# Turning keys, queries and tokens by the DMA crossbar instead of TensorE in a chunked-attention and feed-forward kernel

## The chip, the cores and the metric

The kernel runs on one core of a Trainium2 chip. The metric is the time of one execution on the device in microseconds (us); lower is better. A profile of one execution belongs to each kernel: it shows when each engine worked on which instruction and what it waited for. The engines are TensorE (PE, with its weight loads as PEld), VectorE (DVE), ScalarE (ACT), GpSimd (POOL) and SyncE (SP), which here only issues DMA transfers. DMA transfers are issued by SyncE (queue SPq) and by GpSimd (POOLq).

## The reference

Two stages. The first is attention over chunks of 32 queries: each chunk sees 8 memory keys, 16 keys to its left, its own 32 and 8 to its right. There are 4 batches, 8 heads, 768 positions and a head size of 64. The second is a layer norm and a two-layer feed-forward (512 to 2048 to 512) with a residual.

```python
for c in range(nc):                              # 24 chunks of 32
    l_start = max(0, c_start - 16); r_end = min(S, c_end + 8)
    k_full = np.concatenate([mem_k, k[:, :, l_start:r_end]], axis=2)
    v_full = np.concatenate([mem_v, v[:, :, l_start:r_end]], axis=2)
    scores = scale * np.matmul(q_c, k_full.transpose(0, 1, 3, 2))
    scores = scores - np.max(scores, axis=-1, keepdims=True)
    a = np.exp(scores); a = a / (np.sum(a, axis=-1, keepdims=True) + 1e-09)
    out[:, :, c_start:c_end] = np.matmul(a, v_full)
# x = attention's output, (4, 768, 512)
xn = (x - mu) / np.sqrt(var + 1e-06) * g_ln
out = x + np.maximum(xn @ w_ch1, 0.0) @ w_ch2
```

All inputs and outputs are fp32; the kernel casts to fp16 while it loads.

## The kernel before

Two chunks make a group of 64 queries; there are 12 groups in a batch. A group's scores come from 96 key columns: 8 of memory and 88 around the 64 queries. The keys stand turned (head size on partitions) in `KT`, with two heads on the 128 partitions, four pairs `j`. The queries stand turned in `QZ`, each head in its own half of the partitions and zeros in the other half, so that one matmul gives both heads of a pair. Two groups make a tile of 128 tokens, three tiles a unit of 384 tokens; there are 8 units, two for each batch. While unit `u` goes through the feed-forward, the three tiles of unit `u + 1` go through attention, at steps that a plan lays down. A unit has 28 steps: 16 `up` steps (four matmuls each, then a ReLU, by VectorE at even steps and ScalarE at odd ones), then 12 `down` steps (four matmuls each).

Turning is TensorE's, with an identity, into PSUM; a copy then takes it to SBUF:

```python
def turn_kq(pv, src, j, n):
    for r in range(8):
        for par in range(2):
            nc.tensor.matmul(
                out=pv[64 * par : 64 * par + 64, n * r : n * r + n],
                lhsT=src[0:n, 2 * j + par, r, :], rhs=identity[0:n, 0:n],
                is_transpose=True, start=True, stop=True, tile_position=(0, 64 * par))

def kq_block(b, j, g0, g1, kind):        # keys and queries of two head pairs, j and j + 1
    ...
    for i in range(2):
        turn_kq(as16(pk[:, i, :]), k16[b % 2], j + i, 96)
    for i in range(2):
        turn_kq(as16(pq[i]), q16[b % 2], j + i, 96)
    def keep(i):
        keep_k(...)                      # VectorE: PSUM to KT
        for par in range(2):
            keep_q(nc.scalar.copy, ...)  # ScalarE: PSUM to QZ
    ...

def turn_x(u, i, t, kind="att"):         # a tile's tokens, 128 x 512
    pv = as16(slot("att")[:, 0, :]) if kind == "att" else as16(slot("mm")[:, :])
    for dt in range(4):
        nc.tensor.matmul(
            out=pv[:, 128 * dt : 128 * dt + 128],
            lhsT=xn[t % 3][:, 128 * dt : 128 * dt + 128], rhs=identity,
            is_transpose=True, start=True, stop=True)
    nc.scalar.copy(out=xT[u % 2][:, :, 128 * i : 128 * i + 128], in_=free(pv, 0, [[128, 4], [1, 128]]))
```

Attention of a tile is `scores` (8 matmuls, then two exponentials by ScalarE), `values` (16 matmuls), `norm` (VectorE: reciprocal, scaling with the row sum, mean, and `xn`, the centred row times the gain `g_row`), `turn_x`, and `root` (ScalarE squares, GpSimd makes `rstd`). The feed-forward and the end of a tile:

```python
def up(u, n, hc):
    p = slot("mm")[:, 0 : 128 * n]
    for dt in range(4):
        nc.tensor.matmul(out=p, lhsT=free(w, i, [[4, 128]]), rhs=xT[u % 2][:, dt, 0 : 128 * n], ...)
    if hc % 2: nc.scalar.activation(out=rT[hc][...], in_=p, func=ACTF.Relu)
    else:      nc.vector.tensor_scalar(out=rT[hc][...], in0=p, scalar1=0.0, op0=ALU.max, ...)

def down(t, i, part):
    for hc in range(4 * part, 4 * part + 4):
        nc.tensor.matmul(out=p, lhsT=rT[hc][:, 128 * i : 128 * i + 128], rhs=w2c[hc // 4][:, hc % 4, :], ...)
    if part == 3:
        nc.vector.scalar_tensor_tensor(out=osb[t % 3], in0=p, scalar=rstd[t % 9], in1=xs[t % 9], ...)
        nc.sync.dma_start(out=out[...], in_=osb[t % 3])
```

PSUM has two buffers `att` of two banks each and four `mm` of one. `stay_busy(n)` puts `n` filler matmuls of 512 columns on TensorE. The part of the plan that the change touches:

```python
late = ((16, 19, 19, 22), (17, 21, 21, 24), (19, 23, 23, 26))   # scores, values, norm, turn_x
if u == 0:
    at(1, clear_q, 1, 0); at(5, clear_q, 1, 1); at(8, clear_v, 1); at(11, clear_k, 1)
    for j in (0, 2):
        at(10 + j, kq_block, 0, j, 6, NG, "att"); at(11 + j, keep_rest)
    ...
    attend(late)
elif u == 1:
    for j in (0, 2):
        at(5 + 3 * j, kq_block, 1, j, 0, NG, "att"); at(7 + 3 * j, keep_rest)
    ...
    attend(late)
elif u in (2, 4):
    attend(((1, 8, 8, 12), (4, 8, 10, 14), (11, 17, 17, 21)))
    b = u // 2 + 1
    for j, step in ((0, 17), (2, 23)):
        at(step, kq_block, b, j, 0, NG, "mm"); at(step, keep_rest)
    for h in range(H):
        at(2 + 2 * h, load_v_head, b, h)
    at(21, mem_cols, b); at(21, v_mem, b); at(22, v_around, b)
elif following:                                                   # units 3, 5, 6
    attend(((12, 17, 17, 21), (14, 17, 17, 22), (18, 23, 23, 26)))
```

Of the kernel before, what the change touches and what calls it, by code (L numbers as in the profile page):

```python
# [15 lines left out]
def kernel(  # L16
# [12 lines left out]
    nc = tc.nc  # L29
# [4 lines left out]
    KR = 96  # L34
    KC = NG * KR + 32
    HD = 80
# [21 lines left out]
    w2c = [sb.tile([128, 4, 512], FP16, name=f"w2c{i}") for i in range(4)]  # L58
    k16 = [sb.tile([96, H, 8, 64], FP16, name=f"k16_{i}") for i in range(2)]
    q16 = [sb.tile([96, H, 8, 64], FP16, name=f"q16_{i}") for i in range(2)]  # L60
    V = [sb.tile([128, NG, H, HD], FP16, name=f"V{i}") for i in range(2)]
    KT = [sb.tile([128, 4, KC], FP16, name=f"KT{i}") for i in range(2)]
    QZ = [sb.tile([128, 4, NG, 2, 64], FP16, name=f"QZ{i}") for i in range(2)]
    AT = [sb.tile([128, 2, H, 64], FP16, name=f"AT{i}") for i in range(3)]
# [30 lines left out]
    def as16(t):  # L95
        return t.bitcast(FP16)
# [13 lines left out]
    def load_v_group(b, g):  # L110

        lo, hi = max(64 * g - 16, 0), min(64 * g + 72, S)
        r = 24 + lo - 64 * g
        nc.gpsimd.dma_start(  # L114
            out=V[b % 2][r : r + hi - lo, g, :, 0:64],
            in_=dram(v, b * H * HS + lo * D, [[64, hi - lo], [HS, H], [1, 64]]),
        )

    def load_v_head(b, h):
        nc.gpsimd.dma_start(  # L120
            out=V[b % 2][24:88, :, h, 0:64],
            in_=dram(v, (b * H + h) * HS, [[64, 64], [64 * 64, NG], [1, 64]]),
        )

    def v_around(b):

        vt = V[b % 2]
        nc.sync.dma_start(out=vt[8:24, 1:NG, :, :], in_=vt[72:88, 0 : NG - 1, :, :])
        nc.sync.dma_start(out=vt[88:96, 0 : NG - 1, :, :], in_=vt[24:32, 1:NG, :, :])

    def v_mem(b):
        src = memv16[:, b, :, :]
        nc.sync.dma_start(
            out=V[b % 2][0:8, :, :, :],
            in_=bass.AP(tensor=src.tensor, offset=src.offset,
                        ap=[list(src.ap[0]), [0, NG], [1, H * HD]]),
        )
# [26 lines left out]
    def mem_cols(b):  # L164
        src = memKT[:, 4 * b : 4 * b + 4, :]
        nc.vector.tensor_copy(
            out=free(KT[b % 2], 0, [[KC, 4], [KR, NG], [1, 8]]),
            in_=bass.AP(tensor=src.tensor, offset=src.offset,
                        ap=[list(src.ap[0]), [8, 4], [0, NG], [1, 8]]),
        )  # L170
# [13 lines left out]
    def keep_k(pv, b, j, n, g0, g1, copy=nc.vector.tensor_copy):  # L184

        for ga, gb in ((0, 1), (1, NG - 1), (NG - 1, NG)):
            ga, gb = max(ga, g0), min(gb, g1)
            if ga < gb:
                lo = 0 if ga == 0 else 8 * ga - 2
                m = 10 if gb == NG else 8 * ga + 9 - lo  # L190
                copy(  # L191
                    out=free(KT[b % 2], j * KC + 24 + 32 * ga + 8 * lo,
                             [[KR, gb - ga], [8, m], [1, 8]]),
                    in_=free(pv, lo, [[8, gb - ga], [1, m], [n, 8]]),
                )

    def keep_q(copy, pv, b, j, par, n, g0, g1):


        rows = slice(64 * par, 64 * par + 64)  # L200
        copy(  # L201
            out=free(QZ[b % 2][rows, j, g0, par, :], 0, [[128, g1 - g0], [8, 8], [1, 8]]),
            in_=free(pv[rows, :], 8 * g0, [[8, g1 - g0], [1, 8], [n, 8]]),
        )
# [24 lines left out]
    def keep_rest():  # L229
        kept_later.pop(0)()  # L230

    def scores(b, t):
        p = slot("att")
        a = AT[t % 3]
        for gg in range(2):
            g = 2 * t + gg
            for j in range(4):
                nc.tensor.matmul(  # L238
                    out=p[:, gg, 128 * j : 128 * j + 128],
                    lhsT=KT[b % 2][:, j, KR * g : KR * g + 128],  # L240
                    rhs=QZ[b % 2][:, j, g, :, :],
                    start=True, stop=True,
                )
# [48 lines left out]

    def turn_x(u, i, t, kind="att"):
        pv = as16(slot("att")[:, 0, :]) if kind == "att" else as16(slot("mm")[:, :])
        for dt in range(4):
# [72 lines left out]
    def clear_k(i):  # L368
        nc.vector.memset(KT[i][:, :, 8:24], 0.0)
        nc.vector.memset(KT[i][:, :, NG * KR - 8 : KC], 0.0)  # L370

# [32 lines left out]
    for h in (0, 4):  # L404
        for which in range(2):
            load_kq(0, which, 0, CUT, h, h + 4)
    keep(counts[:, 0:1], counts[:, 0:1], 24, 0.0)
    keep(counts[:, 1:2], counts[:, 1:2], -88, 0.0)
    make_identity(nc, identity)
# [7 lines left out]
    mem_cols(0)  # L417
    pg = slot("mm")[:, :]
    nc.tensor.matmul(out=pg, lhsT=ones32, rhs=g_one, start=True, stop=True)
    nc.scalar.copy(out=g_row, in_=pg)  # L420
    v_mem(0)
# [5 lines left out]
    nc.gpsimd.memset(zero2[:, 1:2], -NEG)  # L427
    keep(band[:, 0:1], zero2[:, 0:1], -64, NEG)
    keep(band[:, 1:2], zero2[:, 0:1], 40, NEG)
    keep(zero2[:, 1:2], zero2[:, 1:2], -8, 0.0)  # L430
    nc.gpsimd.tensor_tensor(out=band[:, 1:2], in0=band[:, 1:2], in1=zero2[:, 1:2], op=ALU.add)
    for g in range(4, 6):
# [47 lines left out]
    scores(0, 1)  # L480
    stay_busy(5)
    values(0, 0)
# [20 lines left out]
    for u, tiles in enumerate(units):  # L503
# [6 lines left out]

        def attend(steps):

            for i, (s0, s1, s2, s3) in enumerate(steps):
# [3 lines left out]
                at(s2, norm, t % 6, t % 9)  # L517
                at(s3, turn_x, u + 1, i, t % 6)
                at(min(s3 + 1, 27), root, t % 6, t % 9)

        late = ((16, 19, 19, 22), (17, 21, 21, 24), (19, 23, 23, 26))
        if u == 0:
            at(1, clear_q, 1, 0)
            at(5, clear_q, 1, 1)
            at(8, clear_v, 1)
            at(11, clear_k, 1)
            for j in (0, 2):
# [5 lines left out]
            for g in range(6):  # L533
                at(15, load_v_group, 1, g)
            attend(late)
            at(26, mem_cols, 1)
            at(26, v_mem, 1)
        elif u == 1:
# [3 lines left out]
            for g in range(6, NG):  # L542
                at(0, load_v_group, 1, g)
            for which in range(2):
                at(1, load_kq, 2, which)
            attend(late)
        elif u in (2, 4):
            attend(((1, 8, 8, 12), (4, 8, 10, 14), (11, 17, 17, 21)))
            b = u // 2 + 1
            for j, step in ((0, 17), (2, 23)):  # L550
                at(step, kq_block, b, j, 0, NG, "mm")
                at(step, keep_rest)
            for h in range(H):
                at(2 + 2 * h, load_v_head, b, h)
            at(21, mem_cols, b)
            at(21, v_mem, b)
            at(22, v_around, b)
        elif following:
            attend(((12, 17, 17, 21), (14, 17, 17, 22), (18, 23, 23, 26)))
            if u == 3:  # L560
                for which in range(2):
                    at(2 + which, load_kq, 3, which)
        for step in range(16 + 4 * n):
# [43 lines left out]
```

## Time and profile before

| | |
|---|---|
| time, median of 3 runs | 233.54 us (230.09 to 233.69) |
| time of the profiled execution, its span | 230.39 us, 228.7 us |
| TensorE clock granted | 1.00 |
| DMA queue of GpSimd (`q0`) | 45680 packets, 14.23 MB |
| DMA queue of SyncE (`q1`) | 4602 packets, 7.54 MB |
| output writes of 256 KB, issue to landing | 4.0 us, median |

A profile is read from the whole to the part. The span runs from the first instruction to the last. Busy time of an engine is the time in which it had an instruction; of TensorE it says little about speed, because matmuls are pipelined, and two that follow each other overlap in the records: the mean duration of a matmul is longer than the step to the next. The chain of waits is followed back from the last instruction, at each step to what released it; its rows are the time that sets the end. Lines are named by their number in the kernel: L176 is a transpose in `turn_kq`, L296 one in `turn_x`, L319 a matmul of `up`, L336 one of `down`, L238 of `scores`, L258 of `values`, L310 a filler.

### The profile page before, as it was taken

How to read it: one execution, taken by the hardware profiler on the slowest of the kernel's cores; microseconds unless marked ns; L12 is line 12 of the kernel's file. 1: busy time of each engine (PE TensorE's matmuls, PEld its weight loads, DVE VectorE, ACT ScalarE, POOL GpSimd, SP SyncE). 2: the span in 40 equal slices, each digit the busy share in tenths (PEclk: the TensorE clock that was granted, in tenths of full speed). 3: DMA queues.
4: the chain of work that ended last, by engine and by line, in shares of the span. 5: the costliest groups of instructions: out<-in, count | busy, mean ns of one | idle time of the engine just before them, and what ended most of it. 6: DMA issues, size and time to landing. Idle time of an engine off the chain costs nothing.

```text
span 228.7 us, 5500 instructions
## 1 busy us (share of the span) xinstructions
PE 221.6 (97%) x2289; PEld 137.2 (60%) x2289; DVE 127.2 (56%) x290; ACT 119.0 (52%) x228; POOL 68.5 (30%) x125
## 2 busy tenths in 40 slices
PE   7989989999999999999999999999999999999993
PEld 2555666557755676556765676556764566556553
DVE  6856882585728548674436557774336532663222
ACT  3565548364884567654356458653446345533200
POOL 7982426968300460440001461310001100030000
PEclk9999999999999999999999999999999999999999
DMA  4999999999995190559911290553001200111012
GB/s 78 181 144 206 211 193 177 178 185 210 122 201 119 67 128 3 37 99 132 241 25 49 90 108 1 37 109 112 0 3 46 92 3 0 47 49 46 0 46 96
DMA packets 50307, 22.13 MB, mean 97 GB/s; under 512 B 37817, under 2 KB 46777, under 8 KB 50234
## 3 DMA queue, kind: packets, MB, share of 16 engines
q0 software_dynamic: 45680, 14.23, 58.4%
q1 hardware_dynamic: 4602, 7.54, 11.0%
q8 instruction: 18, 0.29, 0.6%
q14 instruction: 7, 0.06, 0.1%
HBM read 28.48 MB, written 6.29 MB: 152 GB/s over the span
## 4 chain that ended last, share of the span: by engine, by line
PE 87%; DVE 6%; DMA 3%; issue 2%; POOL 1%; DVEq 0%; POOLq 0%
PE mm L336 35%; PE mm L319 33%; PE att L238 5%; PE att L258 3%; PE att L176 3%; DMA k<-in_k_dram 3%; PE att L296 2%; PE mm L176 2%; PE mm L354 2%; DVE rT L327 1%; DVE xs L269 1%; PE mm L310 1%; DVE xn L278 1%; DVE QZ L374 1%; DVE V L380 1%
## 5 line engine op out<-in xcount | busy, mean ns | idle before, releaser
L319 PE MATMUL mm<-xT,w1c 128*128 128x384 f16 x512 | 88.3, 326 | 0.0
L336 PE MATMUL mm<-w2c,rT 128*128 128x512 f16 x368 | 87.4, 379 | 0.0
L319 PEld LDWEIGHTS <-w1c 128*128 128x128 f16 x512 | 56.6, 113 | 24.5 <-issue 0.3
L327 DVE TENSOR_SCALAR rT<-mm 128x384 f16<-128x384 f32 x64 | 35.3, 554 | 34.7 <-PE mm L319 34.5
L336 PEld LDWEIGHTS <-rT 128*128 128x128 f16 x368 | 33.7, 98 | 33.7
L325 ACT ACTIVATE rT<-mm 128x384 f16<-128x384 f32 x64 | 31.2, 489 | 35.8 <-PE mm L319 33.9
L287 POOL TENSOR_SCALAR veps<-squares 128x1 f32<-128x1 f32 x24 | 4.5, 188 | 115.9 <-ACT junk L284 101.2
L245 ACT ACTIVATE AT<-att,band 96x512 f16<-96x512 f32 x48 | 30.1, 677 | 17.0 <-PE att L238 16.6
L343 DVE SCALAR_TENSOR_TENSOR osb<-mm,rstd,xs 128x512 f32<-128x512 f32 x23 | 17.2, 749 | 30.7 <-PE mm L336 20.1
L114 POOL DMA_DIRECT2D V<-in_v_dram x24 | 21.4, 898 | 10.4 <-DMA w1c<-in_moe_w_ch_dram 5.7
L301 ACT COPY xT<-att 128x512 f16<-128x512 f16 x21 | 12.2, 581 | 22.4 <-PE att L296 22.4
L191 DVE COPY KT<-att 128x80 f16<-128x80 f16 (+3 forms) x44 | 18.4, 480 | 2.4 <-PE att L176 2.4
L278 DVE SCALAR_TENSOR_TENSOR xn<-xs,nmean,g_row 128x512 f16<-128x512 f32 x24 | 18.0, 752 | 0.9
L201 ACT COPY QZ<-mm 64x768 f16<-64x768 f16 (+1 forms) x18 | 13.6, 757 | 7.9 <-PE mm L176 7.7
L284 ACT ACTIVATE junk<-xs,nmean 128x512 f16<-128x512 f32 x24 | 17.4, 724 | 0.1
L268 DVE RECIPROCAL rec<-att 128x8 f32<-128x8 f32 x24 | 4.8, 202 | 22.2 <-PE att L258 22.2
L269 DVE SCALAR_TENSOR_TENSOR xs<-att,rec 128x512 f32<-128x512 f32 x24 | 16.6, 691 | 0.8
L238 PE MATMUL att<-QZ,KT 128*128 128x128 f16 x192 | 14.8, 219 | 0.9 <-ACT AT L245 0.7
L238 PEld LDWEIGHTS <-KT 128*128 128x128 f16 x192 | 12.6, 98 | 4.6 <-issue 1.5
L201 ACT COPY QZ<-att 64x384 f16<-64x384 f16 (+1 forms) x20 | 12.0, 598 | 5.9 <-PE att L176 5.7
L291 POOL TENSOR_TENSOR rstd<-veps,mhalf 128x1 f32<-128x1 f32 x24 | 13.3, 553 | 2.0
L120 POOL DMA_DIRECT2D V<-in_v_dram x16 | 12.1, 763 | 0.3 <-issue 0.3
(63 smaller groups left out, 141.6 us busy)
## 6 DMA issues: line engine op xcount, KB each, us to landing
out_dram<-osb SPq DMA_DIRECT2D x23, 256.0 KB, 4.0
w1c<-in_moe_w_ch_dram POOLq DMA_DIRECT2D x4, 512.0 KB, 10.9
w2c<-in_moe_w_ch_dram POOLq DMA_DIRECT2D x4, 512.0 KB, 14.4
V<-in_v_dram POOLq DMA_DIRECT2D x20, 88.0 KB, 9.8
k<-in_k_dram POOLq DMA_DIRECT2D x2, 768.0 KB, 10.0
q<-in_q_dram POOLq DMA_DIRECT2D x2, 768.0 KB, 13.1
V<-in_v_dram POOLq DMA_DIRECT2D x16, 96.0 KB, 3.2
k<-in_k_dram POOLq DMA_DIRECT2D x3, 256.0 KB, 6.3
```

The source lines that it names most:

```text
L114: nc.gpsimd.dma_start(out=V[b % 2][r : r + hi - lo, g, :, 0:64], in_=dram(v, b * H * HS + lo * D, [[64, hi - lo], [HS, H], [1, 64]]),)
L191: copy(out=free(KT[b % 2], j * KC + 24 + 32 * ga + 8 * lo, [[KR, gb - ga], [8, m], [1, 8]]), in_=free(pv, lo, [[8, gb - ga], [1, m], [n, 8]]),
L201: copy(out=free(QZ[b % 2][rows, j, g0, par, :], 0, [[128, g1 - g0], [8, 8], [1, 8]]), in_=free(pv[rows, :], 8 * g0, [[8, g1 - g0], [1, 8], ...
L238: nc.tensor.matmul(out=p[:, gg, 128 * j : 128 * j + 128], lhsT=KT[b % 2][:, j, KR * g : KR * g + 128], rhs=QZ[b % 2][:, j, g, :, :], start ...
L245: nc.scalar.activation(out=free(a, 32 * c, [[512, 2], [64, 8], [1, 32]], KR), in_=free(p, 32 * c, [[512, 2], [64, 8], [1, 32]], KR), func= ...
L269: nc.vector.scalar_tensor_tensor(out=x.rearrange("p (h d) -> p h d", h=H), in0=free(p, 0, [[128, H], [1, 64]]), scalar=1.0, in1=free(r, 0, ...
L278: nc.vector.scalar_tensor_tensor(out=xn[i], in0=x, scalar=nmean[i], in1=g_row, op0=ALU.add, op1=ALU.mult,)
L284: nc.scalar.activation(out=junk, in_=xs[xi], func=ACTF.Square, bias=nmean[i], accum_out=squares[i],)
L319: nc.tensor.matmul(out=p, lhsT=free(w, i, [[4, 128]]), rhs=xT[u % 2][:, dt, 0 : 128 * n], start=(dt == 0), stop=(dt == 3),)
L325: nc.scalar.activation(out=o, in_=p, func=ACTF.Relu)
L327: nc.vector.tensor_scalar(out=o, in0=p, scalar1=0.0, scalar2=None, op0=ALU.max)
L336: nc.tensor.matmul(out=p, lhsT=rT[hc][:, 128 * i : 128 * i + 128], rhs=w2c[hc // 4][:, hc % 4, :], start=(hc == 0), stop=(hc == 15),)
```

## The change

What it does:

- Keys and queries of batches 2 and 3 are loaded by tokens (128 tokens on the partitions, fp16, six loads of keys and six of queries for a batch), and transposing DMA transfers on SyncE's queue turn them: keys straight into `KT`, queries into `QT`, a dense buffer.
- GpSimd copies the queries from `QT` into `QZ` between the zeros (`spread_q`), and copies the 16 and 8 key columns at each group's edges from its neighbours (`k_around`).
- Tokens of units 3 to 7 are turned by a transposing DMA from `xn` to `xT`; those of units 0 to 2 still go by TensorE.
- Units 2 and 4 do the attention of the next unit in their first half (the `up` steps); units 3, 5 and 6 begin it earlier than before.
- To fit the crossbar, `KT` and `QZ` are laid out by group first and head pair second, the 8 memory columns move from the front of a group's 96 to its end (rows of `V` and the masks with them), and batches 2 and 3 hold even groups before odd ones.
- At the start, the matmul that spreads the gain row moves behind the first scores, and its copy from ScalarE to VectorE; in unit 0 the clearing of the second `V` buffer moves from step 8 to step 16.

It is meant to take work from TensorE and from the engines that empty PSUM, and give it to the DMA engines and GpSimd. The diff, cut to its core:

```diff
+    def place(b, g):
+        return g if b < 2 else g % 2 * (NG // 2) + g // 2
+    def load_tokens(b, which, t):
+        dst, src = ((kraw[0], k), (qraw[0], q))[which]
+        nc.gpsimd.dma_start(
+            out=free(dst, 512 * t, [[64, H], [1, 64]]),
+            in_=dram(src, b * H * HS + 128 * t * D, [[D, 128], [HS, H], [1, 64]]))
+    def cross_k(b, half, t0, t1):
+        nc.sync.dma_start_transpose(
+            out=free(KT[b % 2], (24 * half + 4 * t0) * KR + 16, [[KR, 4 * (t1 - t0)], [1, 64]]),
+            in_=kraw[0][64 * half : 64 * half + 64, 512 * t0 : 512 * t1])
+    def cross_q(half, t0, t1):
+        nc.sync.dma_start_transpose(
+            out=free(QT, (24 * half + 4 * t0) * 64, [[64, 4 * (t1 - t0)], [1, 64]]),
+            in_=qraw[0][64 * half : 64 * half + 64, 512 * t0 : 512 * t1])
+    def k_around(b, t0, t1):                 # four nc.gpsimd.tensor_copy of edge columns
+    ...
+    def spread_q(b, half, t0, t1):
+        for par in range(2):
+            rows = slice(64 * par, 64 * par + 64)
+            nc.gpsimd.tensor_copy(
+                out=QZ[b % 2][rows, 6 * half + t0 : 6 * half + t1, :, par, :],
+                in_=QT[rows, ...].rearrange("p (t j x) -> p t j x", j=4, x=64))
     def turn_x(u, i, t, kind="att"):
+        if kind == "dma":
+            nc.sync.dma_start_transpose(out=xT[u % 2][:, :, 128 * i : 128 * i + 128], in_=xn[t % 3])
+            return
 ...
-    pg = slot("mm")[:, :]
-    nc.tensor.matmul(out=pg, lhsT=ones32, rhs=g_one, start=True, stop=True)
-    nc.scalar.copy(out=g_row, in_=pg)
+    stay_busy(4)
 ...
     scores(0, 1)
-    stay_busy(5)
+    stay_busy(2)
+    pg = slot("mm")[:, :]
+    nc.tensor.matmul(out=pg, lhsT=ones32, rhs=g_one, start=True, stop=True)
+    nc.vector.tensor_copy(out=g_row, in_=pg)
+    stay_busy(1)
     values(0, 0)
 ...
+        def cross(steps, b, t0, t1, t2):
+            for half in range(2):
+                at(steps[half], cross_k, b, half, t0, t1)
+                at(steps[2 + half], cross_q, half, t2 - 3, t2)
 ...
-            at(8, clear_v, 1)
-            at(11, clear_k, 1)
+            at(14, clear_k, 1)
+            at(16, clear_v, 1)
 ...                                                   # unit 1
-            for which in range(2):
-                at(1, load_kq, 2, which)
-            attend(late)
-        elif u in (2, 4):
-            attend(((1, 8, 8, 12), (4, 8, 10, 14), (11, 17, 17, 21)))
-            b = u // 2 + 1
-            for j, step in ((0, 17), (2, 23)):
-                at(step, kq_block, b, j, 0, NG, "mm")
-                at(step, keep_rest)
 ...
+            for t in range(6):
+                for which in range(2):
+                    at(14, load_tokens, 2, which, t)
+            attend(((16, 19, 19, 22), (17, 19, 20, 23), (21, 23, 23, 26)), "att")
         elif following:
-            attend(((12, 17, 17, 21), (14, 17, 17, 22), (18, 23, 23, 26)))
 ...
+            if u in (2, 4):
+                attend(((2, 7, 7, 7), (4, 7, 8, 8), (9, 13, 13, 13)))
+            else:
+                attend(((9, 14, 14, 14), (11, 14, 15, 15), (16, 20, 20, 20)))
+            if u == 2:
+                cross((0, 0, 1, 1), 2, 0, 4, 3)
+                at(8, mem_cols, 2)
+                at(8, k_around, 2, 0, 4)
+                for h in range(H):
+                    at(8, load_v_head, 2, h)
+                spread(9, 2, 0, 3)
+                cross((14, 14, 15, 15), 2, 4, 6, 6)
+            elif u == 3:
+                at(1, v_mem, 2)
+                at(1, v_around, 2)
+                at(4, k_around, 2, 4, 6)
+                spread(5, 2, 3, 6)
+                for t in range(6):
+                    for which in range(2):
+                        at(24, load_tokens, 3, which, t)
+            elif u == 4:
+                for h in range(H):
+                    at(0, load_v_head, 3, h)
+                cross((14, 14, 15, 15), 3, 0, 4, 3)
+                at(17, mem_cols, 3)
+                at(17, v_mem, 3)
+                at(17, v_around, 3)
+                at(22, k_around, 3, 0, 4)
+                spread(23, 3, 0, 3)
+                cross((20, 21, 24, 25), 3, 4, 6, 6)
+            elif u == 5:
+                at(2, k_around, 3, 4, 6)
+                spread(3, 3, 3, 6)
```

## The prediction

> **What bounds the kernel now.** I read the page's busy table and chain first, then busy time in the stretches between unit starts (a unit is 384 tokens; its start is where the chain of waits enters a run of `up` matmuls), then the groups by shape.
>
> ```profile
> span 228.7 us, 5500 instructions
> PE 221.6 (97%) x2289; PEld 137.2 (60%) x2289; DVE 127.2 (56%) x290; ACT 119.0 (52%) x228; POOL 68.5 (30%) x125
> ...
> PE 87%; DVE 6%; DMA 3%; issue 2%; POOL 1%; DVEq 0%; POOLq 0%
> ```
>
> TensorE is 97% busy and is 87% of the chain; nothing else comes near. So what counts is how much work leaves TensorE, provided nothing new makes it wait. The stretches show which units carry it (columns: stretch, length, busy time and count of each engine, clock, DMA):
>
> ```profile
> 21.30:50.52 29.22, 28.30 (x330) 17.80 (x328) 18.31 (x43) 17.48 (x37) 17.80 (x28) 1.00 1.33 191
> 50.52:78.03 27.51, 27.51 (x326) 17.41 (x325) 16.94 (x38) 17.61 (x32) 9.24 (x15) 1.00 1.30 150
> 78.03:105.12 27.09, 27.09 (x325) 17.32 (x324) 16.83 (x39) 17.79 (x33) 10.52 (x18) 1.00 0.66 67
> 105.12:129.15 24.03, 24.03 (x198) 14.67 (x196) 11.77 (x26) 10.77 (x22) 1.49 (x4) 1.00 0.53 110
> 129.15:156.25 27.10, 27.10 (x326) 17.29 (x324) 16.84 (x39) 17.80 (x33) 8.90 (x16) 1.00 0.65 73
> 156.25:180.28 24.03, 24.03 (x199) 14.66 (x196) 11.78 (x26) 10.78 (x22) 1.48 (x4) 1.00 0.10 38
> 180.28:204.31 24.03, 24.03 (x198) 14.67 (x197) 11.77 (x26) 11.25 (x24) 2.22 (x6) 1.00 0.09 34
> 204.31:228.70 24.39, 20.84 (x144) 13.57 (x142) 7.81 (x14) 4.39 (x10) 0.74 (x2) 1.00 0.12 44
> ```
>
> These are units 0 to 7. From unit 1 to unit 6 TensorE has no gap at all. Units 3, 5 and 6 take 24.03 us: `up` and `down`, which the chain shows as 10.40 us for 64 matmuls and 0.86 us for four of 512 columns (12 x 0.865 = 10.4), so 20.8, and attention of three tiles, 3.2. Units 2 and 4 are 3.06 and 3.07 us longer; they also turn the keys and queries of batches 2 and 3. Unit 0 is 1.7 us longer than unit 1, with 0.9 us of it a real gap.
>
> **What one turn costs.** The groups by shape give durations that overlap; the chain gives what TensorE's order pays.
>
> ```profile
> 144.34 0.68 PE att L176 x32
> 145.02 0.68 PE mm L176 x32
> ...
> 151.21 0.80 PE att L176 x32
> 152.01 0.68 PE mm L176 x32
> ```
>
> That is unit 4: 128 little transposes, 2.84 us; the rest of its 3.07 is the switch to and fro and short waits for banks. For a token tile, the timeline of unit 3:
>
> ```profile
> 122.66 0.39 PE L296 MATMUL att<-identity,xn 128*128 128x128 f16 x4
> 122.88 1.03 PE L336 MATMUL mm<-w2c,rT 128*128 128x512 f16 x4
> 123.08 0.59 ACT L301 COPY xT<-att 128x512 f16<-128x512 f16 x1 [1.56 <-PE att L296]
> ```
>
> The next matmul begins 0.22 us after the first transpose: 0.22 us of TensorE for a tile (four transposes at 55 ns), not 4 x 219 ns.
>
> **What the Trainium skill says.** "VectorE: DVE Perf Modes", section "The three transpose paths", gives 390 ns for a 128x128 turn on TensorE and 1309 ns by the DMA crossbar. The trace has 219 ns as the time of one on TensorE and 55 ns as the step from one to the next, so the page's first figure is a latency here, and I take the second to be mostly latency too; no crossbar transfer is in this trace. "DMA: Bandwidth & Descriptors", section "Latency and other measured facts", has 261 GB/s measured for a transposing DMA. By it I estimate 0.5 us for a token tile's 128 KB and 1.0 us for 256 KB of keys. The fixed part I take from this trace's writes of 256 KB, 4.0 us from issue to landing, so 3 to 4 us for a tile. "GPSIMD Engine Reference", section "Performance versus the Vector engine", has 769 ns for 512 elements in a tight one-input loop; a spread of 768 is then an estimated 1.2 us, and the trace has no copy on GpSimd to check it against.
>
> **The change, part by part.**
>
> 1. Keys and queries of batches 2 and 3 leave TensorE: 256 transposes in four blocks. By the unit lengths, 3.06 + 3.07 = 6.1 us, all on the path.
> 2. Tokens from unit 3 on: 15 tiles x 4 transposes leave. 15 x 0.22 = 3.3 us, all on the path. Sum so far 9.4 us. ScalarE loses 15 copies of 0.58 us and VectorE the key copies of both batches, neither of which was on the path there.
> 3. Unit 0: clearing the second V buffer (1.34 us and some small ones on VectorE) moves from step 8, in front of the key copies for which TensorE waited 0.9 us, to step 16, where VectorE had 4.9 us of nothing. I give this 1.2 us.
> 4. The start: the gain row's fp32 matmul (1.05 us at 5.6 us) moves between the first scores and the first values; two of five filler matmuls at 0.216 go, so values start about 1.05 - 0.43 = 0.6 us later, a little less if that matmul is quicker there. Behind values the chain is VectorE's, so it passes on: +0.5 us. The four fillers in its old place end before the second half of the keys lands (the chain waits for that until 9.1 us), so they cost nothing.
> 5. New work elsewhere. Token loads: 12 per batch, of 1024 pieces of 256 bytes of source. The V loads of unit 2 are of the same kind:
>
> ```profile
> 79.36 4.48 POOL L120 DMA_DIRECT2D V<-in_v_dram  x6
> ```
>
> Six loads of 768 pieces take GpSimd 4.48 us to issue, and the DMA slices show them running from about 80.85 to 85.95 us, 1.1 ns a piece. So a token load is 1.0 us to issue and 1.13 us to move, twelve are 13.6 us. Begun in step 14 of unit 1 (about 62 us), the fourth key load, seventh in order, lands near 72, and the first key turn is queued at unit 2's start, about 76. In unit 3 they begin near 121 with eight V loads behind them (another 6.8 us): all landed near 144; the first scores that read batch 3 come in unit 5 at about 154. Four spreads are 4.8 us of GpSimd per half batch, and the edge copies less; GpSimd was busy 1.5 us in unit 3. All hidden.
> 6. In units 2 and 4 three attentions move into the `up` half, where VectorE has a ReLU of 0.55 us every 1.3 us; two norms of 1.8 us close together fill about 4 us of it. I allow 0.2 to 0.4 us in each for evictions that come late, 0.8 us with what else may turn up.
>
> Span: 228.7 - 6.1 - 3.3 - 1.2 + 0.5 + 0.8 = 219.4 us. The profiled execution took 230.39 with a span of 228.7, so 1.7 goes on top: 221.1. The timed runs were 230.09, 233.54 and 233.69, so a run may as well be 3 us above the profiled one; I go half way up, 222.5.
>
> **The rivals.**
>
> - *The last token tile comes late.* In units 3, 5 and 6 its norm is at step 20. Seven `down` steps of 0.865, 6.05 us, remain until `up` of the next unit, which needs all 384 columns. The norm chain is 0.21 + 0.69 + 0.08 + 0.15 + 0.75, with gaps 2.0 us (118.63 to 120.55 above), and VectorE may be in an eviction of 0.75. That leaves 3.3 to 4.0 us for the crossbar, against my 3 to 4. If it takes 6 us, three boundaries lose about 2 us each, 6 us in all: 228. For it: the transfer shares the engines with output writes. Against: it is half the bytes of an output write, and stays inside SBUF.
> - *The crossbar's rate is low.* If 1309 ns per 128x128 block were a rate and not a latency, the 1.3 MB queued in unit 2 up to its last token tile (two of 256 KB, two of 192 KB, three tiles of 128 KB, at 32 KB a block 40 blocks) would need 52 us, more than two units, and the tiles, queued last, would hold unit 3 up by 20 to 30 us: 260 and more. Against it stands the page's 261 GB/s.
> - *The queue in order.* Turns, V edge moves and output writes share one queue. In unit 4 the V edges wait for all V loads (about 144 to 147 us) and hold three output writes, but these have three buffers and no successor until about 160 us, so I see no stall. If loads take twice as long, values in unit 5 wait up to 10 us.
> - *TensorE's gain is eaten by banks*: with attention in `up`, VectorE's evictions could hold the four banks. The chain would show ReLU rows; 2 to 3 us, 224.
>
> **Range and chances.** Gains of 9.4 us are counted work on an engine with no gaps; only a new wait can take them. The low end, 218, is every stall absent and runs like the profiled one. The high end, 229, is the first rival in full. Faster by 2% means below about 228.9: 0.84. Within 2%: 0.10. Slower: 0.06, almost all from the second and third rivals.
>
> **What would show it.** Units 2 and 4 at about 23.3 us in place of 27.1, and units 3, 5 and 6 at 23.4 in place of 24.03, with TensorE busy throughout; 140 matmuls fewer in units 2 and 4 and 12 fewer in 3, 5 and 6; unit 0 near 28; the first `up` matmul near 22.5. A wait of TensorE's `up` matmuls for a DMA that writes xT would show the first rival, and its length the crossbar's time; a gap before scores in unit 3 or 5 would show late keys. I am wrong if the units from 2 on are longer than 24 us.

## The result and the profile after

The changed kernel takes 220.04 us (median of 4 runs, 219.87 to 220.25), against 232.56 us before on the same chip: a ratio of 0.950, 95% interval 0.941 to 0.958. Over all the experiments, runs of the kernel before lie between 229.75 and 233.69 us.

The page of the changed kernel, its first lines and its chain:

```profile
span 218.5 us, 4954 instructions
...
PE 212.8 (97%) x1975; PEld 129.2 (59%) x1975; DVE 118.7 (54%) x269; ACT 98.6 (45%) x196; POOL 105.0 (48%) x177
...
PE 90%; DVE 3%; DMA 3%; ACT 1%; issue 1%; POOL 1%; DVEq 0%; POOLq 0%
```

Line numbers in the changed kernel: L374 is `up`, L391 `down`, L288 `scores`, L308 `values`, L351 a token turn by TensorE, L365 a filler; on SyncE's queue L345 turns a token tile, L247 keys and L253 queries (`kraw<-qraw` in the profile), L401 writes output, L130 and L131 move the V edges; on GpSimd L241 loads tokens.

TensorE is as full as before, with 314 matmuls fewer, and ScalarE lost 20 us of work. GpSimd gained 36.5 us without appearing in the chain beyond its 1%. The stretches of units 1 to 7, with the same columns as before the change (length, busy time and count of PE, PEld, DVE, ACT and POOL, clock, DMA):

```profile
50.56:77.84 27.28, 27.28 (x326) 17.55 (x324) 16.86 (x38) 18.39 (x34) 18.83 (x26) 1.00 1.66 146
77.84:101.22 23.38, 23.38 (x186) 14.11 (x184) 11.76 (x27) 9.79 (x22) 16.98 (x31) 1.00 1.18 152
101.22:124.55 23.33, 23.33 (x186) 14.03 (x184) 11.87 (x26) 9.95 (x20) 6.33 (x12) 1.00 0.41 75
124.55:147.90 23.35, 23.35 (x187) 14.05 (x184) 11.68 (x27) 9.31 (x20) 17.16 (x28) 1.00 1.95 167
147.90:171.23 23.33, 23.33 (x186) 14.05 (x185) 12.33 (x26) 9.95 (x20) 10.07 (x18) 1.00 0.54 123
171.23:194.56 23.33, 23.33 (x186) 14.07 (x185) 11.87 (x26) 9.95 (x20) 2.23 (x6) 1.00 0.18 51
194.56:218.50 23.94, 20.84 (x144) 13.61 (x142) 7.81 (x14) 3.93 (x8) 0.00 (x0) 0.98 0.13 45
```

Units 2 to 6 are now alike, 23.33 to 23.38 us, with TensorE busy from end to end of them. The first `up` matmul comes at 22.60 us (21.98 before), and unit 0 takes 27.96 us (28.54 before). So the span's 10.2 us are: 3.71 and 3.75 in units 2 and 4, 0.70 in each of units 3, 5 and 6, 0.58 in unit 0, 0.23 in unit 1, 0.45 at the end, less 0.62 at the start. The 0.45 is not work saved: the stretch from TensorE's last matmul to the end of the span, in which the last output lands, is 3.09 us in place of 3.54.

What the crossbar takes, from the DMA issues of the changed kernel (count, median us from issue to landing; 128 KB for a tile `xT`, up to 256 KB for `KT`, 192 KB for the queries):

```profile
xT<-xn SPq DMA_TRANSPOSE x15, 2.8
...
KT<-kraw SPq DMA_TRANSPOSE x8, 4.2
kraw<-qraw SPq DMA_TRANSPOSE x8, 3.1
```

And the tightest place, the end of unit 3, in the timeline of the changed kernel:

```profile
119.61 0.75 DVE L328 SCALAR_TENSOR_TENSOR xn<-xs,nmean,g_row 128x512 f16<-128x512 f32 x1
...
120.43 1.20 SPq L345 DMA_TRANSPOSE xT<-xn  x1
...
121.37 0.96 POOL L241 DMA_DIRECT2D kraw<-in_k_dram  x1
...
124.39 1.79 PE L374 MATMUL mm<-xT,w1c 128*128 128x384 f16 x10
```

The last token tile is ready at 120.4, its turn is issued at once and lands 2.4 us later, 1.6 to 1.7 us before `up` of unit 4 reads it (124.39 here, 124.55 in the chain). The token loads of batch 3 start 0.9 us after the turn was issued. In other places of this kernel a tile's turn takes up to 5.9 us to land. Whether the order here is luck is what several experiments below ask.

### The profile page after: what moved, and what is told of

Read it like the earlier page. It is cut to its first block, busy times and chain, and to the rows that moved or that the text cites. A ratio compares the mean times of both kernels' runs of the same rounds, so it can differ in the third digit from the quotient of the medians.

```text
span 218.5 us, 4954 instructions
## 1 busy us (share of the span) xinstructions
PE 212.8 (97%) x1975; PEld 129.2 (59%) x1975; DVE 118.7 (54%) x269; ACT 98.6 (45%) x196; POOL 105.0 (48%) x177
## 4 chain that ended last, share of the span: by engine, by line
PE 90%; DVE 3%; DMA 3%; ACT 1%; issue 1%; POOL 1%; DVEq 0%; POOLq 0%
PE mm L374 38%; PE mm L391 37%; PE att L288 5%; PE att L308 3%; DMA kraw<-in_k_dram 3%; PE att L178 2%; PE mm L409 2%; DVE xs L319 1%; ACT QZ L203 1%; DVE xn L328 1%; PE att L351 1%; PE mm L178 1%; PE att L365 1%; DVE QZ L203 1%; PE mm L365 0%
## 5 line engine op out<-in xcount | busy, mean ns | idle before, releaser
L374 PE MATMUL mm<-xT,w1c 128*128 128x384 f16 x512 | 88.5, 327 | 0.0
L391 PE MATMUL mm<-w2c,rT 128*128 128x512 f16 x368 | 84.2, 379 | 0.0
L374 PEld LDWEIGHTS <-w1c 128*128 128x128 f16 x512 | 56.8, 114 | 24.3 <-issue 0.3
L391 PEld LDWEIGHTS <-rT 128*128 128x128 f16 x368 | 34.8, 98 | 37.8
L328 DVE SCALAR_TENSOR_TENSOR xn<-xs,nmean,g_row 128x512 f16<-128x512 f32 x24 | 18.5, 771 | 0.9
L276 POOL COPY QZ<-kraw 64x768 f16<-64x768 f16 x16 | 14.4, 900 | 3.5 <-DMA kraw<-qraw 2.9
L288 PE MATMUL att<-QZ,KT 128*128 128x128 f16 x192 | 14.8, 219 | 0.2 <-DVE QZ L203 0.2
L288 PEld LDWEIGHTS <-KT 128*128 128x128 f16 x192 | 12.6, 98 | 4.0 <-issue 0.3
L365 PE MATMUL mm<-busy 128*128 128x512 f16 x34 | 11.1, 454 | 1.2 <-DVE counts L455 1.2
L268 POOL COPY KT<-KT 128x128 f16<-128x128 f16 (+4 forms) x16 | 4.2, 293 | 15.6 <-DMA KT<-kraw 15.6
L241 POOL DMA_DIRECT2D kraw<-in_k_dram x12 | 11.4, 954 | 0.0
```

What stands on the lines that cost most here:

```text
L288: nc.tensor.matmul(out=p[:, gg, 128 * j : 128 * j + 128], lhsT=KT[b % 2][:, (4 * g + j) * KR : (4 * g + j) * KR + 128], rhs=QZ[b % 2][:, g ...
L328: nc.vector.scalar_tensor_tensor(out=xn[i], in0=x, scalar=nmean[i], in1=g_row, op0=ALU.add, op1=ALU.mult,)
```

## The experiments

The theory: what leaves TensorE leaves the time, one for one, as long as each transfer lands before its reader. Rivals: the gain comes from emptier ScalarE and PSUM, or from where attention stands; the crossbar's lateness eats part of it. In the cuts of the edits `...` marks lines left out. Unit lengths below are from one `up` start to the next.

**Tokens by TensorE again.**

```diff
-                at(min(s3 + 3, 27), root, t % 6, t % 9)
+                at(min(s3 + (1 if u > 1 else 3), 27), root, t % 6, t % 9)
...
-            attend(((2, 7, 7, 7), (4, 7, 8, 8), (9, 13, 13, 13)))        # units 2, 4
+            attend(((2, 7, 7, 11), (4, 7, 8, 12), (9, 13, 13, 17)), "att")
-            attend(((9, 14, 14, 14), (11, 14, 15, 15), (16, 20, 20, 20)))
+            attend(((9, 14, 14, 18), (11, 14, 15, 20), (16, 20, 20, 24)), "att")
```

> The changed kernel with the tokens of units 3 to 7 turned by TensorE again, each three to five steps after its norm as before; keys and queries stay with the crossbar. Theory (the gain is TensorE's own instructions, one for one): 60 transposes come back, 15 tiles x 0.22 us = 3.3 us, so a span near 221.8 and a time near 223.3 us; units 2 to 6 each 0.66 us longer, no gaps of TensorE. Rival A (the gain of the tokens came from ScalarE and PSUM banks being free): 5 us or more come back. Rival B (the crossbar's waits had eaten the tokens' gain): within 0.5 us of the changed kernel's 220.0.

Measured: 224.17 us (223.5 to 224.35), span 222.4. Units 2 and 4 are 24.27 us (0.9 more), units 3, 5 and 6 are 24.0 (0.67 more), TensorE without a gap: 3.8 us for 15 tiles, 0.25 us a tile. The theory holds. The 0.03 us above the prediction's 0.22 come from units 2 and 4. There two of three turns stand among `up` matmuls, and the chain of this run gives them 0.36 and 0.34 us; turns among `down` matmuls take 0.22. In the kernel before, unit 4 shows it for one of its two. Its chain there has these `up` matmuls (start, duration), and the turns fill the gaps between them, 0.38 and 0.22 us:

```profile
139.04 0.65 PE mm L319 x4
140.07 1.30 PE mm L319 x8
141.59 0.65 PE mm L319 x4
```

Why only some of them are longer stays open.

**Tokens alone, in the kernel before.**

```diff
+        if kind == "dma":                 # in turn_x, as in the changed kernel
...
-                at(min(s3 + 1, 27), root, t % 6, t % 9)
+                at(min(s3 + (3 if kind == "dma" else 1), 27), root, t % 6, t % 9)
...
-            attend(((1, 8, 8, 12), (4, 8, 10, 14), (11, 17, 17, 21)))     # units 2, 4
+            attend(((1, 8, 8, 8), (4, 8, 10, 10), (11, 17, 17, 17)), "dma")
...
-            attend(((12, 17, 17, 21), (14, 17, 17, 22), (18, 23, 23, 26)))
+            attend(((9, 14, 14, 14), (11, 14, 15, 15), (16, 20, 20, 20)), "dma")
```

> The kernel before with one part of the change alone: tokens of units 3 to 7 by the crossbar, with the last tile's norm at step 17 in units 2 and 4 and at step 20 in units 3, 5 and 6; keys and queries stay with TensorE. Theory: 3.3 us less than before, a span near 225.4; the keys' part is then the other 6 us and the two add up. Rival A: more than 5 us less. Rival B (a late tile): less than 1.5 us less, with TensorE waiting for a transposing transfer ahead of up in units 4, 6 and 7.

Measured: 226.26 us (225.77 to 227.39), ratio 0.976 (0.968 to 0.984), span 224.6, 4.1 us below the span before. Units 3, 5 and 6 are at 23.33, units 2 and 4 at 26.28 and 26.27, a fall of 3.74 us over the five. What units 2 and 4 still have above the changed kernel, 2.90 and 2.92 us, is the keys' part: 5.8 us. The parts add up, 3.74 + 5.82 = 9.6, and no wait for `xT` is in the trace.

**Units 2 and 4 attend as late as the others.**

```diff
-            attend(((2, 7, 7, 7), (4, 7, 8, 8), (9, 13, 13, 13)))        # units 2, 4
+            attend(((9, 14, 14, 14), (11, 14, 15, 15), (16, 20, 20, 20)))
```

> The changed kernel with units 2 and 4 attending as late as units 3, 5 and 6 do (scores at 9, 11, 16; last norm and turn at step 20). Theory (order in the one transfer queue decides): in unit 4 the last token tile stands behind the V edges, which wait for V loads until about 146 us, and behind an output write: it is turned near 152 and lands near 154.5, so unit 5 starts 5 to 7 us late and the time is 225 to 227 us; unit 2, whose queue has no V edges, stays at 23.4 us. Rival (only the amount of work counts, and where attention stands is indifferent): 220.0, within 0.4 us. Rival (banks): unit 2 changes by as much as unit 4.

Measured: 232.76 us, the whole gain gone. In this run's waits of TensorE (us in all, times, the longest):

```profile
PE mm L374 <- DMA xT<-xn: 10.1, 2, 9.2
```

and its transfer queue in the same time:

```profile
149.75 0.56 SPq L130 DMA_DIRECT2D V<-V  x1
150.36 1.47 SPq L131 DMA_DIRECT2D V<-V  x1
151.93 1.92 SPq L401 DMA_DIRECT2D out_dram<-osb  x1
153.97 2.35 SPq L345 DMA_TRANSPOSE xT<-xn  x1
```

The columns are start, duration, queue, line, transfer. The tile stands behind the V edges and an output write, is issued at 153.97 and lands at 158.2; unit 5 starts at 158.27 in place of 147.90. The mechanism is the theory's, the size is more: 9.2 us of wait where I expected 5 to 7, and after it unit 5 takes 25.6 us and not 23.3, because the clock granted was 0.66 over its first 6.7 us. The wait for unit 3, which I had thought free of this, was the other 0.9 us. So the early attention of units 2 and 4 is, as far as this run shows, no gain by itself; it is what keeps the token tiles ahead in a queue that runs in order.

**The last tile four steps later, and two steps later.**

```diff
-            attend(((9, 14, 14, 14), (11, 14, 15, 15), (16, 20, 20, 20)))
+            attend(((9, 14, 14, 14), (11, 14, 15, 15), (20, 24, 24, 24)))    # four; two: (18, 22, 22, 22)
```

> The changed kernel with the last tile of units 3, 5 and 6 four steps later (scores 20, values, norm and turn at step 24). In the changed kernel's trace its turn is issued at 120.43, takes 2.4 us to land, and up begins at 124.55: 1.7 us to spare. Four down steps are 3.46 us, so theory: TensorE waits 1.8 us ahead of up three times, 5.3 us in all, a time near 225.3 us, and the wait is for the transfer that writes xT. Rival (the crossbar can keep up with anything, slack is larger than the trace shows): within 0.5 us of 220.0. Rival (output writes ahead of it in the queue add their time): 3 us each, 229.

> The changed kernel with the last tile of units 3, 5 and 6 two steps later (scores 18, values, norm and turn at step 22). Two down steps are 1.73 us, as much as the 1.7 us to spare in the trace. Theory: at the edge, 0 to 0.4 us each, a time of 220.0 to 221.2 us. Rival (slack is smaller, since other transfers delay it): 1 us each or more, 223 and over.

Measured: 232.67 us with four steps (231.61 to 234.03), 225.99 with two (224.57 to 227.72). Both are worse than the theory. At two of the three boundaries it holds: with four steps TensorE waits 3.7 us at the two together where 1.8 each was expected, and with two steps units 5 and 6 are 23.60 us, 0.27 over, as expected of the 1.7 us to spare. But with two steps unit 3 takes 27.33 and unit 4 26.07. The waits, the timeline and the stretches of that run (the profiled execution is the longest of its six, 227.72 us):

```profile
PE mm L374 <- DMA xT<-xn: 3.8, 1, 3.8
```

```profile
117.30 0.96 POOL L241 DMA_DIRECT2D kraw<-in_k_dram  x1
...
126.93 0.97 POOL L241 DMA_DIRECT2D qraw<-in_q_dram  x1
```

```profile
122.34 1.20 SPq L345 DMA_TRANSPOSE xT<-xn  x1
```

```profile
128.58:133.00 4.42, 4.42 (x18) 2.36 (x19) 0.94 (x2) 0.49 (x1) 3.90 (x6) 0.50 2.18 189
133.00:140.00 7.00, 7.00 (x82) 4.97 (x80) 3.13 (x9) 4.11 (x8) 2.28 (x4) 0.91 2.01 125
```

The token loads for batch 3 ran from 117.30 on, and the turn, issued at 122.34 in the midst of them, let TensorE wait 3.8 us; then the clock stood at 0.50 for 4.4 us and more (the column before the DMA share). With four steps the same turn took 7.4 us to land, and TensorE waited 6.8 us there. The Trainium skill, "DMA: Bandwidth & Descriptors", section "Issuing engines are not separate DMA queues", says that transfers from all engines run on the same 16 DMA engines and interleave; here that is 2.4 us alone and 7.4 us among token loads. And "TensorE: Matmul & The Clock Gate", section "Part 1: The HAM clock gate (the "warmup" mystery)", says that TensorE goes to half clock after an idle window of about 3.4 us and takes one busy window to return. With four steps the trace, cut into half microseconds, is close to that: half clock about 3.5 us after the last matmul, full clock about 3.5 us after the first one of unit 4. With two steps it differs: half after about 2.6 us, full after about 5.6. So the clock fell sooner here than the page has it, and stayed down longer.

Why did the loads start earlier than in the changed kernel? In the plan they stand at step 24, and a tile's `root` three steps after its norm: at 23 in the changed kernel, at 25 here. GpSimd takes them in this order, so in the changed kernel the loads are held back by the last tile's `root`, which needs that tile's squares. The next run asks this.

**Token loads behind the last root.** The two-step version, with one thing more:

```diff
-                        at(24, load_tokens, 3, which, t)
+                        at(26, load_tokens, 3, which, t)
```

> The run with the last tile two steps later (norm and turn at step 22), with one thing more: the token loads of batch 3 stand at step 26 of unit 3 in place of 24, so that in GpSimd's order they come behind the last tile's root and not before it. In that run they began at 117.30 us, the turn was issued at 122.34 in the midst of them, and TensorE waited 3.8 us for it and then ran at a clock of 0.50 for 4.4 us. Theory (loads in flight make the turn late): unit 3 takes 23.6 us as units 5 and 6 do there, unit 4 is back at 23.4, and the time is 220.8 to 221.2. Rival (unit 3's turn is late for another reason, the output write ahead of it in the queue): 225 to 226 as in that run.

Measured: 221.18 us (221.0 to 221.41), units 3, 5 and 6 at 23.65, 23.60 and 23.61, unit 4 back at 23.34. The timeline of this run has the turn at 122.05 and the first load at 122.98, and the wait is down to

```profile
PE mm L374 <- DMA xT<-xn: 0.2, 1, 0.2
```

The output write stands ahead of the turn in both runs, so the rival is out: 4.8 us hung on whether a group of loads stands before or behind one small instruction in GpSimd's order. That the changed kernel has them behind it is due to the place of its last tile, two steps earlier, and not to the step written for the loads.

**The gain row early again.**

```diff
     mem_cols(0)
-    stay_busy(4)
+    pg = slot("mm")[:, :]
+    nc.tensor.matmul(out=pg, lhsT=ones32, rhs=g_one, start=True, stop=True)
+    nc.scalar.copy(out=g_row, in_=pg)
...
-    stay_busy(2)                # then the gain row's matmul, its copy, stay_busy(1)
+    stay_busy(5)
```

> The changed kernel with the gain row's matmul back at its old place before the first key transposes, its copy on ScalarE, and five fillers before the first values. In the changed kernel's trace values begin at 15.35 us in place of 14.73, and VectorE copies the gain row between 15.13 and 15.82, ahead of the first reciprocal. Theory: the first up matmul comes back from 22.60 to about 22.0 and the time falls by 0.6 us, to 219.4. Rival (the gain row was moved because it delayed the first key transposes or a query copy on ScalarE, which sets the start): no gain or a loss of up to 0.5 us.

Measured: 221.22 us (220.65 to 222.86), 1.2 us more and not 0.6 less; the first `up` at 23.27 us. The same stretches of this run and of the changed kernel:

```profile
8.00:9.30 1.30, 1.21 (x27) 0.60 (x24) 1.26 (x9) 1.16 (x3) 1.15 (x7) 0.92 1.38 190
9.30:12.50 3.20, 3.20 (x45) 1.48 (x41) 1.55 (x5) 1.45 (x4) 3.18 (x5) 0.50 2.06 149
```

```profile
8.00:9.30 1.30, 1.08 (x25) 0.47 (x23) 1.26 (x8) 1.19 (x3) 1.15 (x7) 1.00 1.36 185
9.30:12.50 3.20, 3.20 (x69) 1.84 (x63) 2.47 (x7) 2.37 (x6) 3.18 (x5) 1.00 2.36 143
```

The clock halves from 9.3 to 12.5 us: 45 matmuls in place of 69. The runs also lie 2.2 us apart, those of the changed kernel 0.4 us. The fall is not in every execution: the kernel before has the gain row at the same place, and its profile shows 1.00 in these stretches. Does this explain the scatter of the kernel before?

**The start alone, in the kernel before.** The reverse of that edit, applied to the kernel before.

> The kernel before with one part of the change alone: at the start, four fillers of 512 columns stand where the gain row's fp32 matmul stood, and that matmul comes between the first scores and values with its copy on VectorE. In the run with the gain row early, the granted TensorE clock fell to 0.50 between 9.3 and 12.5 us and five fillers took 2.32 us in place of 1.25. Theory: the early fp32 matmul makes the clock fall in some executions and not in others, which is the scatter of the kernel before (229.7 to 233.7 us); moved, it costs 0.6 us of order and takes the scatter away: runs within 0.8 us of each other, a median of 230.4 to 231.0 us. Rival (the scatter has another source, transfers or memory): the runs spread over 3 us and more as before, median 232.

Measured: 231.03 us, 14 runs from 230.63 to 231.34, while 19 runs of the kernel before spread from 229.92 to 233.69 beside it (median 231.6); the ratio is 0.999 (0.996 to 1.002). The scatter is gone, for 0.3 us on the first `up` matmul in this run's profile. So the move does not make the best run faster, it removes the worse ones. That the clock is the cause is shown only in part. Among the 19 runs of the kernel before, times of 231.3 to 232.8 us go with mean granted clocks of 0.982 to 0.993, where the new start has 0.997 to 1.00; but the four longest, 233.4 to 233.7 us, have 1.00, like those at 230, and what lengthens them stays open. Which half of the edit does it, the fillers in the gap or the fp32 matmul out of it, was not tried.

**Clears early again.**

```diff
-            at(14, clear_k, 1)
-            at(16, clear_v, 1)
+            at(11, clear_k, 1)
+            at(8, clear_v, 1)
```

> The changed kernel with the second buffers of V and K cleared at steps 8 and 11 of unit 0 again, as before. I had put 1.2 us on this move; the unit starts show unit 0 shorter by 0.58 us. Theory: unit 0 goes back from 27.96 to 28.5 us, time 220.6. Rival (the move is worth the 1.2 us and something else in unit 0 took half of it): 221.2. Rival (clearing is hidden either way): 220.0.

Measured: 220.94 us (220.49 to 221.3), unit 0 at 28.38 against 27.80 us by the start of its matmuls in the timeline: 0.58 us, and the wait of TensorE for the key copies is back with 0.9 us. The theory held in unit 0. The medians are 0.9 us apart and the profiled spans 0.8, between the 0.6 of the theory and the 1.2 of the rival; what lies above unit 0's 0.58 stays open.

**Query copies shared between ScalarE and VectorE in unit 0.**

```diff
-                keep_q(nc.scalar.copy, as16(pq[i]), b, j + i, par, 96, g0, g1)
+                copy = nc.vector.tensor_copy if g0 and par else nc.scalar.copy
+                keep_q(copy, as16(pq[i]), b, j + i, par, 96, g0, g1)
```

> The changed kernel with one of the two query copies of each pair in unit 0's key blocks on VectorE in place of ScalarE. The chain of waits of unit 0 runs through four query copies and a ReLU of ScalarE, 2.36 us between 31.45 and 33.77, while VectorE has gaps. Theory (ScalarE's copies are what is left of unit 0's excess over unit 1, 27.96 against 27.28): 0.4 to 0.7 us less, 219.5. Rival (VectorE's key copies and ReLUs then become the wait): no change, or 0.3 us more.

Measured: 220.37 us (220.01 to 220.59), no gain. The wait of 0.2 us for ScalarE's query copies became one of 0.5 us for VectorE's key copies: the same banks are emptied by two engines, and the one that took work over became the late one.

**The gain row by DMA.**

```diff
-    nc.sync.dma_start(out=g_one, in_=dram(moe_g_ln, 0, [[0, 1], [1, 512]]))
...
     v_mem(0)
+    nc.sync.dma_start(out=g_row, in_=dram(moe_g_ln, 0, [[0, 128], [1, 512]]))
...
-    stay_busy(2)                # then the gain row's matmul, its copy, stay_busy(1)
+    stay_busy(5)
```

> The changed kernel with the gain row spread over the partitions by a DMA transfer from memory, issued behind the memory values at about 7.5 us, in place of the matmul and the copy; the four fillers stay, and five stand before the first values. Theory (at the start the order on TensorE and VectorE is the loss, the early matmul was the loss of the other run): first up at about 22.0 us in place of 22.6, no fall of the clock, time 219.4. Rival (the transfer delays the second half of keys or queries, or the gain row lands after 16 us): 220.0 or above.

Measured: 219.94 us (219.73 to 220.16), span 218.1, the first `up` at 22.07 as expected and the clock at 1.00; but the time is the same as 220.04 within the runs. In this run TensorE waited 0.9 us for the first queries to land, and equal starts of other runs have their first `up` between 22.08 and 22.75, so the first `up` alone tells little. From the second block of key transposes, whose start varies with the loads, to the first `up` is a steadier measure: 13.59 us in the changed kernel (9.01 to 22.60) and in the run with the start alone (8.65 to 22.24), 12.87 us here (9.20 to 22.07) and in the kernel before (9.11 to 21.98). So moving the matmul costs 0.72 us of order, and the DMA gives them back; in the times of the runs that does not show.

**Unit 2's tokens by the crossbar too.** With the edit above:

```diff
-                    at(14, load_tokens, 2, which, t)
-            attend(((16, 19, 19, 22), (17, 19, 20, 23), (21, 23, 23, 26)), "att")    # unit 1
+                    at(26, load_tokens, 2, which, t)
+            attend(((15, 18, 18, 18), (16, 18, 19, 19), (19, 21, 21, 21)))
```

> The version with the gain row by DMA, and the tokens of unit 2 turned by the crossbar as well: in unit 1 norms and turns at steps 18, 19 and 21, and the token loads of batch 2 at step 26, behind the last root, as the run with loads behind showed to be needed. Theory: three tiles at 0.25 us leave TensorE in unit 1, which falls from 27.28 to 26.5 us, and the later loads are still in time for unit 3: 0.7 us less, 219.2 us against 219.9 of the version without it. Rival (with key blocks up to step 13, scores at 15 wait for ScalarE's query copies, or the last tile lands late): 219.9 or above. Rival (the later loads hold the transfer queue in unit 2, and its token tiles come late for unit 3): a wait for xT ahead of unit 3, 222 or above.

Measured: 223.65 us (223.27 to 224.17), 3.7 us more than without it. TensorE's waits in this run name the places:

```profile
PE att L308 <- DMA V<-V: 1.5, 1, 1.5
...
PE mm L374 <- DMA xT<-xn: 1.1, 1, 1.1
PE att L308 <- DMA V<-in_v_dram: 0.9, 1, 0.9
PE att L288 <- ACT QZ L203: 0.7, 1, 0.7
```

Both rivals came true. Scores at step 15 wait for ScalarE's query copies, and unit 1 grew to 27.74 us; and with loads from 76.2 us on, key turns begin at 86.9 in place of 79.4, token tiles of unit 3 at 94.0 in place of 86.5, and the V edges come last.

## Why the prediction was right

By its own steps:

1. *Keys off TensorE*: expected 6.1 us, shown 5.8 (units 2 and 4 of the tokens-alone run against the changed kernel).
2. *Tokens off TensorE*: expected 3.3, shown 3.7 to 3.8 in both directions. The 0.22 us was read among `down` matmuls; among `up` matmuls, where two of three turns stand in units 2 and 4, a turn took up to 0.38. So part of what I gave to the keys of units 2 and 4 was the tokens' (0.82 us there for three tiles, 0.70 in the other units): taken together, 9.6 us against my 9.4.
3. *Unit 0*: expected 1.2, shown 0.58. This term was mis-sized by half. I took the whole 0.9 us of wait and more, but behind VectorE's key copies ScalarE's query copies were nearly as late: the chain of the changed kernel runs through them there, and sharing them out gained nothing. And I began unit 0 too early. In the chain of the kernel before, 21.30 is where fillers start:

```profile
21.30 0.65 PE mm L310 x3
...
21.98 0.82 PE mm L319 x4
```

From the first `up`, unit 0 was 1.0 us longer than unit 1 and not 1.7, less than the 1.2 I wanted to take from it.

4. *The start*: expected 0.5 later, shown 0.62 by the first `up` of the profiles and 0.72 by order. Its meaning I did not see: it takes the scatter away.
5. *New work hidden*: right. Token loads took 0.9 to 1.0 us each to issue; spreads took 0.90 us each where I had estimated 1.2. That the loads of batch 3 also stay clear of the last token turn, I had not asked.
6. *0.8 us for late evictions*: not there; TensorE has no gap in units 2 to 6, so the rival of the banks did not come either.

The span came out at 218.5 against 219.4, a gain of 10.2 us where I had 9.3. Some of that nearness is luck: unit 0 gave 0.62 less than I said, the 0.8 kept for evictions was not needed, and 0.68 (unit 1 and the landing of the last output) I had not forecast at all; the cause of unit 1's 0.23 stays open. The large part, the 9.4 us counted on TensorE, is what the experiments confirm. The 1.4 us on top, half way up the scatter of the runs, is the mis-sized term of the time: the scatter belonged to the start of the kernel before, and the change took it away.

Of the rivals, the late tile did not occur in the changed kernel. The room was what I had counted (4.0 us from the turn's issue to `up`, against 3.3 to 4.0) and the crossbar quicker than my 3 to 4, but its 2.4 us hold only with no loads in flight. I named output writes as the danger; the token loads were it. The queue in order did not bite either, because units 2 and 4 turn their tiles before the V edges; I had looked only at the output writes behind those edges, and with late attention it was a token tile behind them that took the whole gain. The rate rival was false: a tile lands in 2.4 us, at most 5.9 in the changed kernel. My estimate used 261 GB/s; a stretch of key and query turns moved 180:

```profile
DMA packets 1817, 0.45 MB, mean 180 GB/s; under 512 B 1817, under 2 KB 1817, under 8 KB 1817
```

This is the changed kernel's DMA between 81.5 and 84 us.

## What to carry to other kernels

When one engine has no gaps, count the time by its order (start to start), not by durations, and what leaves it leaves the span. Read the cost of a step where it stands: the same turn cost 0.22 us among one kind of matmul and up to 0.38 among another. Then ask of each transfer that takes its place what may stand ahead of it in its own queue and what shares its engines at that moment: waits of 3.8, 6.8 and 9.2 us there cost 2.7, 1.7 and 2.3 us more, by a lower clock in the unit behind them. Fix the order of loads against such a transfer on purpose, by placing them behind an instruction that depends on it or on its tile.

## What the runs showed of the hardware

- A transposing DMA keeps SyncE's queue for 1.2 to 1.3 us (medians of the changed kernel: 1.19 for the 128 KB of a tile, 1.25 for 192 KB of queries, 1.28 for keys of up to 256 KB; up to 2.9 in single cases), where an output write of 256 KB takes 0.33 us there (median; up to 1.9). Three tiles in a row thus hold the queue for 3.6 us by this sum (3.87 in the last run above), which I had not counted.
- A token tile's 128 KB landed 2.4 us after its issue with no loads in flight, and 6.1 and 7.4 us after it among token loads of 256-byte pieces.
- After waits of 3.8, 6.8 and 9.2 us the granted clock was 0.50, 0.58 and 0.66 over the next 4.4, 4.2 and 6.7 us. TensorE was busy all that time, at that rate.
- Runs that scatter by 3.8 us can have their cause in the first 15 us: with the same start as the changed kernel, 14 runs of the kernel before lay within 0.7 us.
